# Folding the keys' sums to 64 partitions ahead of one product with ones, in a fused attention and feed-forward kernel

## The chip, the cores and the metric

The kernel runs on one core of one Trainium2 chip. A core has TensorE (PE in the profile; PEld is its weight load), VectorE (DVE), ScalarE (ACT), GpSimd (POOL) and SyncE (SP), which run side by side and wait for each other by semaphores; each takes its own instructions in the order in which they are written. The metric is the device time of one execution in microseconds (us).

## The reference

Linear attention with random features for 8 batches, 8 heads, 576 positions and head size 64, with 128 features, then a feed-forward layer with a residual tanh over 4608 tokens of 512 values:

```python
def phi(x):
    proj = np.einsum('bhsd,md->bhsm', x, omega)
    sq = np.sum(x * x, axis=-1, keepdims=True) / 2.0
    h = proj - sq
    h = h - np.max(h, axis=-1, keepdims=True)
    return np.exp(h) / np.sqrt(m)
q_p, k_p = (phi(q_s), phi(k_s))
kv = np.einsum('bhsm,bhsd->bhmd', k_p, v)
z = np.sum(k_p, axis=2)
num = np.einsum('bhsm,bhmd->bhsd', q_p, kv)
den = np.einsum('bhsm,bhm->bhs', q_p, z)[..., None] + 1e-06
x = num / den                       # then to 4608 x 512
h = x @ w_in                        # 512 -> 2048
out = (h - np.tanh(h)) @ w_out      # 2048 -> 512
```

What matters here is z, the sum over the positions of the keys' features, for each batch, head and feature. It is needed on all 128 partitions, since the denominators are sums over the free dimension of the queries' features times z.

## The kernel before

The tokens are worked on in 9 chunks of 512. The feed-forward layer of one chunk (units f, 16 per chunk) runs while keys and queries of later chunks are prepared. TensorE multiplies in a rounded 32-bit type, so most operands are split into a high part and a low part (the rest), and a product is made of two or three products of parts.

The order of all work is written out by hand in a table of tokens, ORDER. A token names a unit, a step and sometimes buffers: `k20.zh.0` is the step zh of the key unit for batch 2, head pair 0, with buffer 0. The program runs through the table and issues each step's instructions; on each engine they stay in that order. Buffers and PSUM banks are named in the tokens, and waits between engines follow from who writes and reads them.

The first two batches of keys are handled in another form. The other 24 key units (6 batches, 4 head pairs) are made by `k_unit`. In such a unit, 576 positions of two heads are projected, reduced and exponentiated in groups A0, A1, M, B0, B1 (M holds 64 positions of each head, in the two halves of the partitions), multiplied with the values into `pk`, and summed:

- zA and zB (GpSimd, L841 and L842) add the four blocks of a head to `zs`, a place of 128 partitions x 2 heads x 128 features inside the tile `zf`. Each partition holds the sum over the positions that lie on it.
- zM (GpSimd, L846, two instructions of 64 partitions) adds group M.
- zh (VectorE, L851) rounds `zs` to its high part, zl (GpSimd, L854) makes the low part; both stand in the tile `zhl`.
- ca and cv (L858, L861) collect the keys' product with the values out of PSUM.
- kt (TensorE) transposes those (L865) and multiplies a matrix of ones with the high part and with the low part (L867, two products into one PSUM place). That sums over the 128 partitions, with the result on every partition.
- ka, kb, zb, wa, wv take the results out of PSUM.

Other lines of which the text speaks: L682 projections on TensorE (into a PSUM bank that must have been read out before); L693 the reduction on VectorE; L802 and L806 high and low part of the keys' features (VectorE, GpSimd); L820 and L825 those of the values (GpSimd, VectorE); L673 low parts of queries or keys (VectorE); L756, L762, L763, L766, L770 the queries' part with its numerators; L925 the first product of the feed-forward layer (h), L939 tanh and L940 the difference, L929 and L942 its split into zr, L935 to L937 the second product (po); L958 and L960 copy results out.

The tile `zf` is one large tile that holds several things at fixed places: the sums `zs`, the feed-forward layer's working blocks, results that wait to be sent, the identity matrix. So `zf` in a row can be any of these; the line tells which.

Of the kernel before, what the change touches and what calls it, by code (L numbers as in the profile page):

```python
# [127 lines left out]
k32.tM q23.ta0 k32.khA0.1 k32.tA1 q23.z1.5 k32.klA0 k32.eM q23.tv0 x2.h2 f1d.o2 k32.khM.0 q23.a1 k32.kvA0.2 x2.l2 f1e.o1
k32.eA1 q23.l1 f1f.h3 k32.khA1.1 k32.klM q23.m1.6 f1f.th k32.klA1 f1d.o3 q23.ta1 f1f.g k32.vhM.1 k32.kvA1 q23.tv1 f1e.o2
f1f.gh.0 k32.vhB0.0 k32.vlM f1e.o3 x2.h3 k32.zA f20.h0.5 f1f.gl f20.h1 x2.l3 k32.pB0.3 k32.pB1.6 k32.vlB0 k32.cB0  # L130
k32.kvM k33.sa f20.h2 f1f.o0 k32.vhB1.1 k32.tB0 f20.h3 k32.cB1 k32.vlB1 k32.eB0 k33.sv0 k33.lv f21.h0.3 s1.c0.0 k32.tB1
f20.th f21.h1 s1.d0 k32.khB0.1 k33.sv1 k32.eB1 k32.klB0 f21.h2 f20.g k30.ld f21.h3 k32.khB1.0 k32.zB f20.gh.1 k32.kvB0
# [5 lines left out]
q33.p0.0.1 q33.p1.6 q33.c0 f22.o0 q33.c1 q33.t0 k33.kvA1 q33.t1 q33.e0 k33.pB0.0 k33.vhB0.0 f23.h3 k33.vlB0 k33.cB0
q33.d0 q33.e1 k33.pB1.6 f22.o1 k33.tB0 k33.cB1 f23.th k33.tB1 q33.p3.0 k33.kvM k33.eB0 f23.g f22.o2 k33.vhB1.1 q33.c3
k33.vlB1 k33.eB1 q33.p2.6 k33.khB0.0 f22.o3 k30.lv q33.t3 k33.klB0 q33.c2 k33.khB1.1 f23.gh.0 f24.h0.2 k33.zB q33.e3  # L140
q33.t2 k33.kvB0 f23.gl f24.h1 q33.e2 f24.h2 k30.sa k33.klB1 f23.o0 k30.vhA1.0 f23.o1 q30.sa k30.sv0 k33.zM k33.kvB1
f23.o2 k30.vlA1 k33.ca f23.o3 k30.sv1 k30.vhA0.1 k30.pA0.0 f24.h3 k30.cA0 k33.zh.0 k31.ld f25.h0.6 k33.cv f24.th k33.zl
k30.tA0 f25.h1 f24.g k30.eA0 k33.kt k30.vlA0 f24.gh.1 q30.sv f25.h2 k33.ka k33.zb f25.h3 k33.kb k30.pM.0 q32.ld
k30.pA1.2 f24.gl k33.wa f26.h0.3 k30.cM k30.cA1 k30.khA0.1 f25.th k30.tM f24.o0 k30.klA0 q33.d1 k30.eM f24.o1 k30.kvA0.0
f24.o2 k30.khM.0 f25.g k30.vhM.1 f26.h1 k33.wv f25.gh.0 k30.tA1 f24.o3 k30.klM k30.vlM k30.eA1 f26.h2 f25.gl k30.zA
f26.h3 k30.khA1.1 f25.o0 f26.th q33.d3 f25.o1 k30.klA1 f25.o2 f26.g k30.kvA1 k30.pB0.6 k30.vhB0.0 k30.pB1.2 q33.d2
f26.gh.1 f25.o3 k30.vlB0 k30.cB0 q33.rc k30.kvM k31.sa f26.gl f27.h0.3 k30.vhB1.1 q33.n0 f26.o0 q33.n1 k30.vlB1 f27.h1
# [238 lines left out]
def favor_attention_ffn(ctx: ExitStack, tc: tile.TileContext, qT, kT, va, vt, omT, w, out):  # L386
# [395 lines left out]
    def k_unit(b, c):  # L782
# [61 lines left out]
        def z_mid():  # L844
            for h, r in enumerate(halves):
                nc.gpsimd.tensor_add(zs[r, h], zs[r, h], u["phM"][r, 0])  # L846
# [191 lines left out]
```

## Time and profile before

| | |
|---|---|
| median of 3 runs | 1026.26 us (1025.16 to 1032.76) |
| the profiled execution | 1025.03 us, of which the span from the first to the last instruction is 1023.0 us |
| TensorE's granted clock over the span | 0.996 |
| TensorE busy | 1007.6 us (98%) |
| VectorE busy | 780.0 us (76%) |
| ScalarE busy | 685.1 us (67%) |
| GpSimd busy | 329.2 us (32%) |

A row of a group names line, engine, operation, what it writes and reads, shapes and count, then busy time in us, mean length of one in ns, and the engine's idle time just before. A row of a line's or tile's instructions gives minimum, median and maximum length in ns. A row of a timeline gives start and length in us, and in brackets idle time with what ended it; rows that follow each other without a gap are merged (x2). A row of the chain of waits gives the start of a piece of the chain, its length, and the engine and line. A row of a table of stages gives the stretch, its length, and the busy time of TensorE, its weight loads, VectorE, ScalarE and GpSimd. Matmuls are pipelined, so the row of one lasts longer than the time until the next one starts.

The 24 key units of the kind described run from about 155 to 810 us.

### The profile page before, as it was taken

The page shows a single profiled execution, that of the slowest core. Times are in us where ns is not written, and L with a number is a line of the kernel's source. Part 1 is how long each engine was busy: PE and PEld are TensorE (multiplying, and loading weights), DVE is VectorE, ACT ScalarE, POOL GpSimd, SP SyncE. Part 2 cuts the span into 40 slices and gives each one's busy share as a digit, 9 for nine tenths or more (in the row PEclk, how much of TensorE's full clock was granted, in tenths as well). Part 3 has the DMA queues.
Part 4 walks back from the last instruction along what each step waited for, and adds up shares of the span by engine and source line. Part 5 has one row for each costly group of instructions (what it writes and reads, how often), then busy time and mean ns, then how long its engine had stood idle before and what let it go on. Part 6 is the DMA issues. An engine that isn't in the chain of part 4 may idle for free.

```text
span 1023.0 us, 16682 instructions
## 1 busy us (share of the span) xinstructions
PE 1007.6 (98%) x5272; PEld 839.5 (82%) x5272; DVE 780.0 (76%) x2618; ACT 685.1 (67%) x1677; POOL 329.2 (32%) x561
## 2 busy tenths in 40 slices
PE   8799999999999999999999999999999999999998
PEld 7688878888888888888888888888888888888886
DVE  7899768888978898789888997887877868343222
ACT  7977767777866687568676886776856768343222
POOL 2414324552354405550655025512663210000000
PEclk9899999999999999999999999999999999999999
DMA  9944532101111102100220012100210010001001
GB/s 359 412 140 86 141 65 77 54 25 45 42 53 39 34 22 75 47 24 21 65 57 23 24 30 77 36 22 24 76 45 1 22 52 11 1 1 41 1 1 42
DMA packets 24872, 61.78 MB, mean 60 GB/s; under 512 B 2640, under 2 KB 5072, under 8 KB 22736
## 3 DMA queue, kind: packets, MB, share of 16 engines
q1 hardware_dynamic: 23056, 54.81, 16.0%
q0 software_dynamic: 1584, 5.77, 2.9%
q8 instruction: 42, 0.69, 0.3%
q14 instruction: 46, 0.38, 0.1%
q10 hardware_dynamic: 144, 0.13, 0.0%
HBM read 45.50 MB, written 9.44 MB: 54 GB/s over the span
## 4 chain that ended last, share of the span: by engine, by line
PE 86%; DVE 5%; ACT 5%; DMA 2%; POOL 1%; issue 1%; SPq 0%; ACTq 0%; DVEq 0%; POOLq 0%
PE h L925 35%; PE po L935 12%; PE po L937 12%; PE po L936 12%; PE pk_k L834 3%; PE pj_q L682 2%; PE pt_q L748 2%; DMA n_f<-qT 2%; PE pn_q L763 1%; PE pn_q L762 1%; PE pj_k_B L682 1%; ACT phi_q L699 1%; PE pj_k_A L682 1%; DVE zf L730 1%; PE n_pj L554 1%
## 5 line engine op out<-in xcount | busy, mean ns | idle before, releaser
L925 PE MATMUL h<-xa,w 128*128 128x512 f32 x1728 | 440.9, 393 | 0.4 <-DVE nb_k_A L693 0.4
L925 PEld LDWEIGHTS h<-xa,w 128*128 128x128 f32 x1728 | 312.8, 188 | 60.3 <-issue 1.8
L935 PE MATMUL po<-w,zr 128*128 128x512 f32 x576 | 228.3, 396 | 0.0
L937 PE MATMUL po<-w,zr 128*128 128x512 f32 x576 | 225.2, 391 | 0.2 <-DVE zr L942 0.2
L936 PE MATMUL po<-w,zr 128*128 128x512 f32 x576 | 225.0, 391 | 0.0
L942 DVE TENSOR_TENSOR zr<-zf,zr 128x512 fp32r<-128x512 f32 x144 | 106.2, 737 | 69.9 <-ACT zr L929 48.2
L929 ACT CAST zr<-zf 128x512 fp32r<-128x512 f32 x144 | 89.5, 622 | 85.6 <-DVE zf L940 43.8
L940 DVE TENSOR_TENSOR zf<-h,zf 128x512 f32<-128x512 f32 x144 | 98.7, 686 | 54.8 <-ACT zf L939 53.3
L939 ACT ACTIVATE zf<-h 128x512 f32<-128x512 f32 x144 | 85.9, 597 | 76.1 <-PE h L925 49.1
L937 PEld LDWEIGHTS po<-w,zr 128*128 128x128 f32 x576 | 108.1, 188 | 24.6 <-DVE zr L942 0.6
L935 PEld LDWEIGHTS po<-w,zr 128*128 128x128 f32 x576 | 108.3, 188 | 17.4 <-issue 0.3
L936 PEld LDWEIGHTS po<-w,zr 128*128 128x128 f32 x576 | 108.4, 188 | 16.8
L912 POOL TENSOR_TENSOR xa<-xs,xa 128x512 fp32r<-128x512 f32 x16 | 21.3, 1340 | 186.7 <-ACT xa L908 96.7
L699 ACT ACTIVATE phi_q<-phi_q,nb_q 128x128 f32<-128x128 f32 x224 | 75.5, 398 | 4.0 <-DVE nb_q L693 3.0
L806 POOL TENSOR_TENSOR khl_k_A<-phi_Ak,khl_k_A 128x256 fp32r<-128x256 f32 x48 | 37.1, 774 | 123.2 <-DVE khl_k_A L802 115.3
L730 DVE CUSTOM_DVE_ANT_0 zf<-phi_q,zb_k 128x128 bf16<-128x128 f32 (+1 forms) x240 | 66.0, 308 | 2.2 <-ACT phi_q L699 0.6
L693 DVE CUSTOM_DVE_ANT_0 phi_q<-pj_q,phi_q 128x128 f32<-128x128 f32 x224 | 53.6, 284 | 10.5 <-ACT phi_q L688 9.9
L806 POOL TENSOR_TENSOR khl_k_B<-phi_Bk,khl_k_B 128x256 fp32r<-128x256 f32 x48 | 45.5, 947 | 38.6 <-DVE khl_k_B L802 34.0
L688 ACT COPY phi_q<-pj_q 128x256 f32<-128x256 f32 x112 | 39.2, 374 | 19.5 <-PE pj_q L682 18.8
L770 DVE TENSOR_TENSOR xs<-pn_q,xs 64x512 f32<-64x512 f32 x56 | 38.5, 687 | 13.5 <-ACT xs L766 12.3
L766 ACT COPY xs<-pn_q 64x512 f32<-64x512 f32 x56 | 32.6, 582 | 19.2 <-PE pn_q L763 17.8
L756 DVE TENSOR_TENSOR ql_q<-pt_q,qh_q 128x512 fp32r<-128x512 f32 x56 | 38.5, 688 | 8.8 <-ACT qh_q L752 7.8
(151 smaller groups left out, 1726.9 us busy)
## 6 DMA issues: line engine op xcount, KB each, us to landing
raw<-w SPq DMA_DIRECT2D x16, 1024.0 KB, 10.6
...
```

The costliest lines, as they stand in the source:

```text
L693: nc.vector.tensor_tensor_reduce(u[kind][:, at + i], v["pj"][:, i, :M], u[kind][:, at + i], scale=-SCALE, scalar=3.0e38, op0=ALU.add, op1= ...
L699: nc.scalar.activation(u[kind][:, at + i], u[kind][:, at + i], AF.Exp, bias=v["nb"][:, i : i + 1], scale=-1.0)
L730: nc.vector.tensor_tensor_reduce(next(turn)[r], u["ph"][r, i], kvs[b, c][1][r, h], scale=1.0, scalar=EPS, op0=ALU.mult, op1=ALU.add, accum ...
L806: nc.gpsimd.tensor_sub(k[:, :m, 1], u["ph" + g[0]][:, t : t + m], k[:, :m, 0].bitcast(F32))
L925: nc.tensor.matmul(u["p"], w_, x[:, c], start=(c, i) == (0, 0), stop=(c, i) == (NC - 1, 2))
L929: nc.scalar.copy(u["gh"], g)
L935: nc.tensor.matmul(po, u["gh"][:, t], whi, start=f == 0, stop=False)
L936: nc.tensor.matmul(po, u["gh"][:, t], wlo, start=False, stop=False)
L937: nc.tensor.matmul(po, u["gl"][:, t], whi, start=False, stop=f == NF - 1)
L939: st = dict(th=lambda: nc.scalar.activation(g, blocks(u["p"]), AF.Tanh), g=lambda: nc.vector.tensor_sub(g, blocks(u["p"]), g), gh=g_hi, gl ...
L940: g=lambda: nc.vector.tensor_sub(g, blocks(u["p"]), g),
L942: gl=lambda: nc.vector.tensor_sub(u["gl"], g, u["gh"].bitcast(F32)))
```

## The change

A new step zf is put behind zM in all 24 units. VectorE adds partitions 64 to 127 of the sums to partitions 0 to 63 (one instruction of 64 partitions x 256 elements, both inputs in SBUF). The high part is then made of 64 partitions and stands in partitions 0 to 63 of the operand; the low part, of the same 64 partitions, is written to partitions 64 to 127 of the same operand. One product with ones over 128 partitions sums both parts at once, in place of two products. GpSimd's and ScalarE's instructions keep their number and order, TensorE has 24 products fewer, VectorE 24 sums more. All other tokens keep their order; the lines of the table are wrapped anew, so that nearly all of it shows in a diff. Of the table two lines are shown.

```diff
-k20.klB1 f0f.o3 f11.gl k21.ld k22.vhA1.0 k20.kvB1 k20.ca s0.c3.1 f11.o0 f12.th k22.vhA0.1 k20.zM k20.cv s0.d3 k22.pA0.6
...
+k20.klB1 f0f.o3 f11.gl k21.ld k22.vhA1.0 k20.kvB1 k20.ca s0.c3.1 f11.o0 f12.th k22.vhA0.1 k20.zM k20.zf k20.cv s0.d3
...
+        def z_fold():
+            nc.vector.tensor_add(zs[0:D], zs[0:D], zs[D:P])
+
         def z_hi(slot):
             u["zhl"] = ak.tile([P, 2, 2, M], F32R, tag=f"khl{slot}", name=f"zhl_{n}")
             copy = nc.scalar.copy if KH == "A" else nc.vector.tensor_copy
-            copy(u["zhl"][:, 0], zs)
+            copy(u["zhl"][0:D, 0], zs[0:D])
 
         def z_lo():
-            nc.gpsimd.tensor_sub(u["zhl"][:, 1], zs, u["zhl"][:, 0].bitcast(F32))
+            nc.gpsimd.tensor_sub(u["zhl"][D:P, 0], zs[0:D], u["zhl"][0:D, 0].bitcast(F32))
...
-            for i in range(2):
-                nc.tensor.matmul(u["pk"][:, 1].rearrange("p h m -> p (h m)"), ones[:, 0:1].to_broadcast([P, P]),
-                                 u["zhl"][:, i].rearrange("p h m -> p (h m)"), start=i == 0, stop=i == 1)
+            nc.tensor.matmul(u["pk"][:, 1].rearrange("p h m -> p (h m)"), ones[:, 0:1].to_broadcast([P, P]),
+                             u["zhl"][:, 0].rearrange("p h m -> p (h m)"), start=True, stop=True)
...
-        st.update(zA=partial(zsum, 0), zB=partial(zsum, 1), zM=z_mid, zh=z_hi, zl=z_lo, ca=c_hi, cv=c_sum, kt=turned,
+        st.update(zA=partial(zsum, 0), zB=partial(zsum, 1), zM=z_mid, zf=z_fold, zh=z_hi, zl=z_lo, ca=c_hi, cv=c_sum, kt=turned,
```

In the changed kernel's line numbers the fold is L850, and what was L851, L854, L861 and L867 is L855, L858, L865 and L870.

More of the change, by code (lines that the diff above doesn't have):

```diff
@@ L128 @@
[L128 to L132, printed above, removed]
@@ L138 @@
[L138 to L142, printed above, removed]
@@ L143 @@
[L143 to L147, printed above, removed]
@@ new lines @@
+k22.pA0.6 k22.vlA1 f11.o1 k22.vlA0 k22.cA0 f11.o2 k20.zh.0 k22.tA0 k20.zl f11.o3 f12.g k22.eA0 k20.kt f12.gh.1
+k22.khA0.1 k22.pM.6 k22.pA1.5 k22.klA0 k20.ka f12.gl k22.cM k20.zb k22.cA1 q20.d1 f13.th f12.o0 q20.d3 f12.o1 q20.d2
+k20.kb f12.o2 q20.rc k20.wa k22.tM q20.n1 q20.n0 k22.kvA0.3 f12.o3 k20.wv k22.vhM.1 k22.tA1 k22.eM q20.z0.6 f13.g
+k22.eA1 f14.h0.5 k22.khM.0 k22.vlM q20.a0 k22.klM f14.h1 f13.gh.0 k22.zA q20.l0 f14.h2 k22.khA1.1 q20.m0.2 f13.gl
+k22.klA1 q21.p3.6 q20.ta0 f14.h3 q21.c3 q20.tv0 f13.o0 f14.th q21.t3 q20.z1.2 f14.g q21.e3 k22.kvA1 k22.pB0.6 k22.vhB0.0
@@ new lines @@
+f24.o1 k30.kvA0.0 f24.o2 k30.khM.0 f25.g k30.vhM.1 f26.h1 k33.wv f25.gh.0 k30.tA1 f24.o3 k30.klM k30.vlM k30.eA1 f26.h2
+f25.gl k30.zA f26.h3 k30.khA1.1 f25.o0 f26.th q33.d3 f25.o1 k30.klA1 f25.o2 f26.g k30.kvA1 k30.pB0.6 k30.vhB0.0
+k30.pB1.2 q33.d2 f26.gh.1 f25.o3 k30.vlB0 k30.cB0 q33.rc k30.kvM k31.sa f26.gl f27.h0.3 k30.vhB1.1 q33.n0 f26.o0 q33.n1
+k30.vlB1 f27.h1 k30.tB0 k31.lv k31.sv0 f26.o1 k30.cB1 k30.eB0 q33.z0.6 k31.sv1 f27.h2 q33.a0 k30.tB1 k41.ld f26.o2
+k30.khB0.1 k30.eB1 q33.l0 k30.klB0 f27.h3 k30.khB1.0 k30.zB k30.kvB0 f27.th q33.m0.2 f26.o3 f27.g q33.ta0 k31.vhA1.0
@@ new lines @@
+q33.z1.6 k30.klB1 k31.vlA1 f27.gh.0 f28.h0.3 q33.a1 k30.zM k30.zf q33.tv0 k30.kvB1 f28.h1 k30.ca q33.l1 k31.vhA0.1
+q30.p0.2.1 k30.zh.1 f28.h2 k30.cv q30.c0 k30.zl f27.gl q33.m1.6 k30.kt q33.ta1 k31.vlA0 f28.h3 q30.t0 k30.ka k30.zb
+q33.tv1 f27.o0 q30.e0 k30.kb f28.th q30.p1.2 q30.d0 q30.p3.6 k30.wa k31.pA0.0 f28.g q30.c1 f27.o1 q30.c3 k31.cA0 k30.wv
+q30.p2.3 q30.t1 f28.gh.1 f27.o2 k31.tA0 q30.c2 q30.e1 f28.gl k31.pM.2 k31.pA1.0 f27.o3 k31.eA0 q30.t2 q30.d1 f28.o0
+k31.cM q30.e2 f29.h0.3 k31.cA1 k31.tM k31.khA0.0 q32.sa k31.tA1 f29.h1 k31.klA0 q30.t3 f29.h2 q30.d2 q30.e3 q32.sv
@@ new lines @@
+k40.zA f31.o2 f31.o3 f33.h2 f32.gl q41.ld k40.vhM.1 f33.h3 k40.khA1.0 f32.o0 f33.th k40.klA1 k40.vlM f32.o1 k40.kvA1
+k40.pB0.0 f33.g k40.vhB0.0 k40.pB1.6 k40.cB0 k40.kvM k40.vlB0 k43.sa f32.o2 k40.tB0 k40.vhB1.1 k40.vlB1 f32.o3 k43.lv
+f34.h0.7 k40.cB1 k43.sv0 k40.eB0 f34.h1 k43.sv1 f33.gh.0 f34.h2 f33.gl k42.ld f34.h3 k40.tB1 k40.khB0.0 f35.h0.0 k40.eB1
+k40.klB0 f34.th f35.h1 k40.khB1.1 k40.zB f34.g k40.kvB0 f35.h2 f34.gh.1 f35.h3 k43.vhA1.0 f34.gl k40.klB1 f33.o0
+k43.vlA1 f35.th f33.o1 k40.zM k40.zf f35.g k43.pA0.6 k43.pA1.7 k43.cA0 k40.kvB1 f33.o2 k40.zh.0 k43.cA1 k43.vhA0.1
@@ new lines @@
+k43.tA0 k40.ca k40.zl k43.pM.0 k43.vlA0 f33.o3 k43.eA0 k43.cM k40.cv f34.o0 f35.gh.0 k43.tM k43.khA0.1 k40.kt k43.tA1
+k43.eM k43.klA0 f35.gl f34.o1 k43.eA1 k40.ka k43.kvA0.6 k40.zb k43.zA f34.o2 k43.khM.0 f35.o0 k43.khA1.1 f35.o1 k43.klM
+k40.kb k40.wa k43.klA1 f35.o2 k40.wv k43.vhM.1 f34.o3 k43.kvA1 k43.pB0.0 k43.vlM k43.vhB0.0 k43.pB1.7 k43.cB0 f35.o3
+k42.sa k43.tB0 k43.kvM k43.vlB0 f36.h0.2 k43.vhB1.1 k43.vlB1 f36.h1 k43.cB1 k42.sv0 k42.lv k43.eB0 f36.h2 k43.tB1
+k43.khB0.1 f36.h3 k43.eB1 k42.sv1 k43.klB0 f37.h0.0 f36.th k43.khB1.0 k51.ld f37.h1 k43.zB f36.g k43.kvB0 f37.h2
@@ new lines @@
+f36.gh.1 k42.vhA1.0 f37.h3 f36.gl k43.klB1 f38.h0.7 k42.vlA1 f37.th f36.o0 k43.zM k43.zf f37.g k43.kvB1 k42.pA0.2
+f37.gh.0 k42.pA1.0 k42.vhA0.1 k43.zh.1 f36.o1 k43.ca k42.vlA0 k42.cA0 k43.zl f37.gl f36.o2 k42.cA1 f36.o3 k43.cv f38.h1
+k42.tA0 k42.tA1 k42.eA0 k43.kt k42.pM.2 k42.eA1 f38.h2 k42.khA0.0 k42.klA0 k43.ka f38.h3 k42.khA1.1 k43.zb k42.cM k42.zA
+k42.kvA0.0 k43.kb f38.th k42.tM f37.o0 q43.d3 k43.wa k42.eM f37.o1 k42.klA1 f37.o2 k42.khM.0 f37.o3 k42.vhM.1 k43.wv
+f38.g k42.kvA1 k42.pB0.6 q43.d2 f38.gh.1 k42.klM k42.pB1.2 f39.h0.7 k42.cB0 k42.vhB0.0 k51.sa k42.vlM f39.h1 q43.rc
@@ new lines @@
+k42.kvM k42.tB0 f39.h2 q43.n0 k42.vhB1.1 q43.n1 f39.h3 f38.gl q43.z0.6 k42.cB1 k42.vlB1 k42.eB0 f38.o0 k42.tB1 q43.a0
+k42.vlB0 f38.o1 k42.khB0.1 k51.lv k51.sv0 k42.eB1 k42.klB0 f38.o2 f39.th k42.khB1.0 f38.o3 k42.zB q43.l0 k42.kvB0
+f3a.h0.2 f39.g q43.m0.6 k51.sv1 k42.klB1 f39.gh.0 f3a.h1 q43.ta0 f39.gl k50.ld q43.z1.7 k51.vhA1.0 f3a.h2 q43.a1 q43.tv0
+k42.kvB1 k42.zM k42.zf f3a.h3 k42.ca q43.l1 q40.p0.6.1 k42.cv k51.vhA0.1 f3a.th f39.o0 k42.zh.1 q40.c0 k51.vlA1 k42.zl
+f3a.g q43.m1.7 f39.o1 q40.t0 q43.ta1 k51.vlA0 k42.kt q40.e0 q43.tv1 q40.p1.2 q40.p3.6 k42.ka q40.d0 k42.zb q40.p2.7
@@ new lines @@
+k50.khM.0 k51.ca f40.h2 s3.d2 k50.cA0 k50.vhA0.1 k50.cA1 f40.h3 k50.tA0 k50.klM k51.cv k50.eA0 f41.h0.3 k50.vlA1
+k50.vlA0 f40.th s3.c3.1 k51.kt f41.h1 f40.g s3.d3 k51.ka k51.zb k51.kb f41.h2 f40.gh.1 k50.khA0.1 k50.tA1 k50.klA0
+k51.wa f41.h3 f40.gl k50.eA1 k50.kvA0.2 f42.h0.1 k50.zA k50.khA1.1 f41.th f40.o0.6 f41.g f40.o1.5 k50.klA1 k51.wv
+f41.gh.0 f40.o2.0 k50.vhM.1 f41.gl k50.kvA1 k50.pB0.7 k50.pB1.4 k50.cB0 f41.o0 k50.vhB0.0 k53.sa k50.vlM f41.o1 k50.tB0
+k50.kvM k50.vlB0 f41.o2 k50.cB1 k53.sv0 k50.vhB1.1 k50.eB0 f40.o3.3 k50.tB1 k50.vlB1 f41.o3 k50.eB1 k53.sv1 k53.lv
@@ new lines @@
+q60.sv k60.cA1 f4e.o2 f4f.gh.0 f4e.o3 k60.eM k60.tA1 q61.ld k60.khM.0 f51.h0.2 k60.eA1 f4f.gl k60.klM q62.d2 f51.h1
+f50.th k60.zA f4f.o0 f4f.o1 f50.g s4.c0.0 k60.khA1.1 f4f.o2 f50.gh.1 s4.d0 s4.c1.1 k60.klA1 f4f.o3 f50.gl s4.d1 k60.kvA1
+k60.pB0.7 k60.vhB0.0 k60.pB1.1 k60.cB0 f50.o0.6 k60.vlB0 k62.sa k60.tB0 k60.kvM f50.o1.5 k60.vhB1.1 s4.c3.0 f50.o2.7
+k60.cB1 k60.vlB1 k60.eB0 s4.d3 k62.sv0 f50.o3.3 k62.lv s4.c2.1 k62.sv1 f51.h2 s4.d2 k60.tB1 f51.h3 k63.ld k60.khB0.1
+k60.eB1 f52.h0.0 k60.klB0 f51.th k60.khB1.0 f52.h1 k60.zB f51.g k60.kvB0 f52.h2 f51.gh.0 k62.vhA1.0 f52.h3 f51.gl
@@ new lines @@
+f53.gh.0 k62.vlB1 f54.h2 k62.eB1 k62.khB0.1 k63.lv f53.gl k62.klB0 f54.h3 k62.khB1.0 f53.o0 f54.th k62.zB k63.sv1
+k62.kvB0 f53.o1 f53.o2 f54.g k61.ld f53.o3 k63.vhA1.0 f54.gh.1 k62.klB1 k63.vlA1 f55.h0.1 k62.zM k62.zf f54.gl k62.kvB1
+k63.pA0.2 k62.ca k63.pA1.4 k63.cA0 f55.h1 k62.cv k63.cA1 k63.tA0 k63.vhA0.1 f55.h2 k62.zh.1 k63.eA0 k63.vlA0 k62.zl
+k63.tA1 k63.pM.2 f55.h3 k63.cM k63.khA0.0 k63.eA1 k62.kt k63.tM k63.klA0 f55.th f54.o0 k63.khA1.1 k62.ka k63.zA k62.zb
+k62.kb k63.kvA0.4 k63.eM f55.g f54.o1 k62.wa k63.khM.0 f55.gh.0 f54.o2 k63.klA1 k62.wv f54.o3 k63.klM f55.gl k63.kvA1
@@ new lines @@
+q62.ta1 q60.d0 q60.p1.0 f57.h3 k63.ka q62.tv1 q60.c1 k63.zb f56.o2 k63.kb f57.th q63.d3 k63.wa q60.p3.1 q60.t1 q60.p2.4
+q60.c3 q63.rc f56.o3 k63.wv q60.c2 q63.n0 q63.n1 f58.h0.0 q60.t2 q60.t3 f58.h1 q60.e2 f57.g q63.z0.4 q60.e3 q60.d2
+f58.h2 q63.a0 q60.d3 k61.pA0.1 q60.e1 f58.h3 q63.l0 f57.gh.0 q60.d1 f59.h0.2 k61.cA0 f57.gl q61.sa q63.m0.4 q60.rc
+f57.o0 k61.tA0 q60.n0 q60.n1 q63.z1.1 q61.sv f59.h1 f57.o1 q63.a1 q63.ta0 q63.l1 f59.h2 q70.ld f58.th q63.tv0 f57.o2
+k61.eA0 f58.g q63.m1.1 k61.khA0.0 q61.p0.4.1 f58.gh.1 q60.z0.0 k61.klA0 q63.ta1 f59.h3 f58.gl q60.a0 f57.o3 q63.tv1
```

425 lines of the change are left out of this document (193 added, 232 removed).

## The prediction

> **What bounds the kernel now.** I read the page's busy times and its chain first, then the busy time by stage, then the chain of waits around one edited place, then the timelines of sampled places.
>
> ```profile
> PE 1007.6 (98%) x5272; PEld 839.5 (82%) x5272; DVE 780.0 (76%) x2618; ACT 685.1 (67%) x1677; POOL 329.2 (32%) x561
> PE 86%; DVE 5%; ACT 5%; DMA 2%; POOL 1%; issue 1%; SPq 0%; ACTq 0%; DVEq 0%; POOLq 0%
> 160.00:400.00 240.00, 239.01 (x1226) 199.60 (x1225) 206.93 (x770) 179.55 (x462) 101.20 (x181) 1.00 0.16 47
> 600.00:810.00 210.00, 209.63 (x1073) 177.35 (x1072) 170.76 (x633) 146.44 (x375) 91.95 (x162) 1.00 0.12 38
> ```
>
> TensorE (PE) sets the time: 98% busy, 86% of the chain. Between 160 and 810 us, where all 24 edited units lie, it shows almost no idle time (columns of the stage rows: PE, weight loads, VectorE, ScalarE, GpSimd busy). But a matmul's row lasts longer than its turn, so small waits hide in that busy time, and VectorE (DVE) is loaded too: 206.93 of 240 us. The chain at the first edited place, unit k20, tells more:
>
> ```profile
> 179.88 0.42 POOL zf L846
> 180.35 0.67 DVE vhl_k_A L825 x2
> 181.03 0.28 DVE zhl_k L851
> 181.73 0.61 DVE zf L940
> 182.36 0.63 ACT zr L929
> 183.02 0.93 DVE zr L942
> 183.99 0.50 PE po L937
> ```
>
> Here the time runs not through PE but from GpSimd's (POOL's) sum L846 through VectorE and ScalarE to the matmul L937. At this place nothing covers a microsecond added to VectorE.
>
> **What is removed: one product with ones per unit.**
>
> ```profile
> 182.49 0.48 PE L867 MATMUL pk_k<-zhl_k,ones 128*128 128x256 f32 x2
> 182.81 0.28 PE L682 MATMUL pj_k_M<-om,x_k 128*128 128x256 f32 x1
> ```
>
> The two products last 0.48 us together, one such product 0.28, so the second starts 0.20 after the first: 24 x 0.20 = 4.8 us of PE time at most. It counts only until PE's next wait for another engine, as at L937 above, so its worth lies between 0 and 4.8. I take 40%, 1.9 us, since the places below show VectorE's results ending several of PE's waits.
>
> The Trainium skill ("TensorE: Matmul & The Clock Gate", section "Wait — 56ns, not 53.3ns?") gives a warm matmul its columns over 2.4 GHz and about 2.5 ns. For 256 columns that is an estimate of 0.109 us, 2.6 us for 24, and by it the term would be 1.0 instead of 1.9. The trace's 0.20 decides.
>
> **What is added: a fold on VectorE that waits for GpSimd.** Each unit gets one sum of 64x256 with both inputs in SBUF. Its length is bounded by the sums of two SBUF inputs with 128 and 512 elements per partition:
>
> ```profile
> L825 DVE TENSOR_TENSOR vhl_k_A<-v_k,vhl_k_A x48: 275/292/850, 157.3 to 772.3; 128x128 fp32r<-128x128 f32 x48
> L942 DVE TENSOR_TENSOR zr<-zf,zr x144: 640/693/1680, 65.1 to 1013.3; 128x512 fp32r<-128x512 f32 x144
> L846 POOL TENSOR_TENSOR zf<-zf,phi_mk x48: 449/462/981, 179.8 to 798.8; 64x128 f32<-64x128 f32 x48
> ```
>
> Between 0.28 and 0.69 us (minimum/median/maximum stand in ns); a third of the way gives 0.41 for 256 elements. Alone that is 24 x 0.41 = 10 us of VectorE time in a stretch that has 20% idle.
>
> The larger part is where it stands. VectorE takes its instructions in order, and the fold is put right behind GpSimd's sums in the written order, so everything behind it waits for them. Before, the first reader, L851, came later:
>
> ```order
> L958 COPY zf_68<-po_0_3_942 128x512
> L861 TENSOR_TENSOR c1_k2_0_2028<-pk_k2_0_1898,c1_k2_0_2028 128x256
> L825 TENSOR_TENSOR vhl_k2_2_A1_2024<-v_k2_2_1986,vhl_k2_2_A1_2024 128x2x64
> L825 TENSOR_TENSOR vhl_k2_2_A0_2035<-v_k2_2_1986,vhl_k2_2_A0_2035 128x2x64
> L851 CAST zhl_k2_0_2054<-zf_68 128x256
> ```
>
> That is VectorE before, around k20's split of the sums (zhl). And after:
>
> ```order
> L961 COPY zf_68<-po_0_3_942 128x512
> L850 TENSOR_TENSOR zf_68<-zf_68 64x256
> L865 TENSOR_TENSOR c1_k2_0_2028<-pk_k2_0_1898,c1_k2_0_2028 128x256
> L826 TENSOR_TENSOR vhl_k2_2_A1_2024<-v_k2_2_1986,vhl_k2_2_A1_2024 128x2x64
> L826 TENSOR_TENSOR vhl_k2_2_A0_2035<-v_k2_2_1986,vhl_k2_2_A0_2035 128x2x64
> L855 CAST zhl_k2_0_2055<-zf_68 64x256
> ```
>
> The fold (L850) has moved the dependence on GpSimd three instructions forward; the sum c1 and both value splits now queue behind it. At k30 (326 us) it is the same with other work behind it, xs and ql:
>
> ```order
> L826 TENSOR_TENSOR vhl_k3_1_A1_3823<-v_k3_1_3767,vhl_k3_1_A1_3823 128x2x64
> L850 TENSOR_TENSOR zf_68<-zf_68 64x256
> L771 TENSOR_TENSOR xs_97<-pn_q3_3_0_3813,xs_97 64x512
> L757 TENSOR_TENSOR ql_q3_3_1_3850<-pt_q3_3_1_3825,qh_q3_3_1_3837 128x512
> L855 CAST zhl_k3_0_3857<-zf_68 64x256
> ```
>
> Without the L850 row this is the row order before.
>
> To price the wait I take every sixth of the 24 places: units k20, k30, k51, k63. In the timelines below (start, length, engine, line) the POOL rows are the two sums L846, and the first DVE row at a place is what the fold now stands in front of, except where said.
>
> ```profile
> 434.95 1.04 POOL L846 TENSOR_TENSOR zf<-zf,phi_mk 64x128 f32<-64x128 f32 x2
> 436.03 0.29 DVE L851 CAST zhl_k<-zf 128x256 fp32r<-128x256 f32 x1 [0.22 <-POOL zf L846]
> 325.92 0.51 DVE L825 TENSOR_TENSOR vhl_k_A<-v_k,vhl_k_A 128x128 fp32r<-128x128 f32 x1
> 179.84 1.12 POOL L846 TENSOR_TENSOR zf<-zf,phi_mk 64x128 f32<-64x128 f32 x2
> 180.01 0.43 DVE L861 TENSOR_TENSOR c_k<-pk_k,c_k 128x256 f32<-128x256 f32 x1 [0.35 <-ACT c_k L858]
> 326.25 1.04 POOL L846 TENSOR_TENSOR zf<-zf,phi_mk 64x128 f32<-64x128 f32 x2
> 326.36 0.67 DVE L770 TENSOR_TENSOR xs<-pn_q,xs 64x512 f32<-64x512 f32 x1
> 327.99 0.40 PE L682 MATMUL pj_q<-om,x_q 128*128 128x256 f32 x2
> 498.04 0.98 POOL L846 TENSOR_TENSOR zf<-zf,phi_mk 64x128 f32<-64x128 f32 x2
> 499.10 0.74 POOL L806 TENSOR_TENSOR khl_k_B<-phi_Bk,khl_k_B 128x256 fp32r<-128x256 f32 x1
> 500.22 0.29 DVE L693 CUSTOM_DVE_ANT_0 phi_mk<-pj_k_M,phi_mk 128x128 f32<-128x128 f32 x1 [1.81 <-ACT phi_mk L688]
> 656.11 0.98 POOL L846 TENSOR_TENSOR zf<-zf,phi_mk 64x128 f32<-64x128 f32 x2
> 656.72 0.93 DVE L942 TENSOR_TENSOR zr<-zf,zr 128x512 fp32r<-128x512 f32 x1
> 659.09 0.41 DVE L861 TENSOR_TENSOR c_k<-pk_k,c_k 128x256 f32<-128x256 f32 x1
> 659.65 0.41 PE L865 MATMUL pk_k<-zf,c_k 128*128 128x128 f32 x2
> ```
>
> From the first three rows: VectorE starts 0.03 after GpSimd's sums end (435.99 to 436.03), and starts its next instruction 0.07 before the last one ends (326.43 against 326.36). So the work behind a fold starts 0.03 + 0.41 - 0.07 = 0.37 us after the sums end, if VectorE stood waiting, or 0.34 later than now if it didn't.
>
> - k20: sums end 180.96, next work would start 181.33 instead of 180.01: 1.32 late. The chain quoted first runs through this work without a gap to PE, so PE loses 1.3.
> - k30: sums end 327.29, L770 would start 327.66 instead of 326.36: 1.30 late. Its end frees the PSUM bank for the projection at 327.99, which now has 327.99 - 327.03 = 0.96 us; some 0.05 of it is the signal's way, so PE loses 0.4.
> - k51: sums end 499.02, but VectorE idles until 500.22: nothing lost.
> - k63: L942 ends at 657.65, after the sums (657.09), so only 0.34 is added. The transposes at 659.65 need L861's result of 659.50; with 0.05 for the signal 0.10 is free, and PE loses 0.24.
>
> Together 1.94 us at four places out of 2.96 us of VectorE's delay (two thirds passes on), six times that for 24: 11.6 us. Per place the bounds are 0 and 1.3, so 0 and 31 us.
>
> **What else moves.** z_hi and z_lo work on 64 partitions; L846 (64 partitions, 128 elements) takes 0.46 like the full-height sums beside it, so I count no gain. One edit relieves: L846 takes up to 0.98 us instead of 0.46 where VectorE's two-input sums run beside it, and a VectorE that stands behind the fold no longer does that. The page of groups bounds it:
>
> ```profile
> L846 POOL TENSOR_TENSOR zf<-zf,phi_mk 64x128 f32<-64x128 f32 x48 | 25.9, 540 | 1.8
> ```
>
> 48 x (540 - 462) ns = 3.7 us over all, two thirds of which would reach PE: 0 to 2.5. Some of that blocking comes from work ahead of the fold and stays; I take 0.7.
>
> **Sum.** +11.6 - 1.9 - 0.7 = +9.0 us. The profiled execution took 1025.03 us (span 1023.0), the median of three runs 1026.26. So 1034 for an execution like the profiled one and **1035.3 us** against the median, 0.9% slower. Below 1% (1016 to 1036.5) a measurement of this kernel hardly tells a change from none.
>
> **Rivals.**
>
> The fold is hidden, and the kernel is a little faster. VectorE idles 20 to 25% of its time, and PE has work queued, so delays of about a microsecond are taken up before a matmul needs the result, as at k51. Then 1026.3 less 2 to 4.8 is 1021.5 to 1024. It decides where most results have over 1.3 us to spare; against it three of four places stand. Chance 0.16.
>
> Contention makes it worse. The fold reads two SBUF inputs while GpSimd goes on to its next instruction, and such pairs hold each other up: L942 takes 640 to 1680 ns, L846 449 to 981. At k51 L806 (0.74) follows the sums by 0.08 us. If GpSimd gets in first, the fold waits up to 0.74; with half of that, 0.37, at 24 places and two thirds passing on, 24 x 0.37 x 0.67 = 6 us more: 1041. Against it: the fold should start some 0.05 us before L806. Chance 0.17.
>
> The Trainium skill ("SBUF — State Buffer", section "Who interferes with whom") says that a VectorE instruction with two SBUF inputs and a GpSimd instruction that reads SBUF exclude each other, and the first blocks the second completely. By that rule the fold pays or GpSimd does, but one of them always; the trace's stretched rows agree.
>
> The product frees nothing. PE's turns may be set by VectorE at the kt step anyway, and the 4.8 us go into the next wait. Then 1026.3 + 11.6 - 0.7 = 1037. Chance 0.12.
>
> **How the numbers follow.** Forecast 0.55, spread by the sampling of four places to some 1028 to 1040. Hidden 0.16, contention 0.17, nothing freed 0.12. The range 1025 to 1042 leaves out most of the hidden case and the top of the contention case. Slower by over 1% (above 1036.5): all of the contention case, two thirds of the nothing-freed case, 0.4 of the forecast's: 0.47. Faster by over 1% would need 10 us where 4.8 are removed: 0.02. Within 1%: 0.51.
>
> **What would show it.** Right: a fold row of about 0.41 us; VectorE idle ahead of it in some 20 places, ended by POOL zf, about 0.9 us each; PE waits at k20 and at the projection of k30 grown by about 1 and 0.4 us; a single product in the place of L867's pair, the next matmul 0.20 earlier behind it. Wrong: folds that start with no idle time ahead; a fold of 0.7 us or more; GpSimd's rows behind the sums longer by the fold's length with PE waiting for them; or PE's busy time down by 4.8 us and the span with it.

## The result and the profile after

The changed kernel takes 1036.95 us (median of six runs, 1035.91 to 1045.02) where the kernel before, run beside it, takes 1025.81 (1025.16 to 1032.76). The ratio is 1.0111, with a 95% interval of 1.0084 to 1.0138: 11.1 us slower, where 9.0 slower (1035.3) was forecast. Now and then an execution of either kernel is 6 to 8 us longer, at a lower clock (1045.02 at 0.986 of full speed over the span, the others of that kernel at 0.994 to 0.996); ratios take these in and medians hardly do, and in the table of the experiments the two differ by up to 2 us.

The profiled execution is the slowest of the six: 1045.02 us, span 1043.2. Its extra 8 us lie in the first stage, before the first fold, as the clock's row (PEclk) and the rows by stage show. First the page: busy times, clock, shares of the chain.

```profile
PE 1020.4 (98%) x5248; PEld 844.8 (81%) x5248; DVE 784.0 (75%) x2642; ACT 684.5 (66%) x1677; POOL 330.2 (32%) x561
PEclk8699999999999999999999999999999999999999
PE 73%; DVE 10%; ACT 7%; POOL 6%; issue 2%; DMA 2%; ACTq 0%; POOLq 0%; SPq 0%; DVEq 0%
```

Then the rows by stage (stretch, its length, busy time of PE, weight loads, VectorE, ScalarE and GpSimd, granted clock, DMA share, GB/s); the first stage of the kernel before stands by itself.

```profile
0.00:160.00 160.00, 150.88 (x990) 123.15 (x991) 133.61 (x333) 124.55 (x285) 52.09 (x69) 0.98 0.60 194
```

```profile
0.00:160.00 160.00, 151.15 (x948) 123.90 (x949) 127.00 (x317) 117.62 (x271) 47.21 (x65) 0.91 0.61 192
160.00:400.00 240.00, 236.76 (x1195) 195.71 (x1194) 203.65 (x748) 175.12 (x446) 99.49 (x177) 1.00 0.15 42
600.00:810.00 210.00, 207.56 (x1053) 173.68 (x1052) 170.59 (x615) 145.73 (x370) 87.06 (x155) 1.00 0.13 38
```

The clock is 0.91 up to 160 us, where it was 0.98, and 1.00 behind it. GpSimd's sums of the first changed unit, k20, start at 188.86 us against 179.84 before: 9.0 late before the change can act.

```profile
188.86 0.99 POOL L847 TENSOR_TENSOR zf<-zf,phi_mk 64x128 f32<-64x128 f32 x2
```

The span is 20.2 longer, so 11.2 us arise behind that point, which agrees with the 11.1 of the medians. So positions inside this profile are compared from one event to the next, not by their time from the start.

In the two later stages shown, PE's idle time went from 0.99 to 3.24 us and from 0.37 to 2.44. In the chain, PE fell from 86% to 73%, VectorE rose from 5 to 10% and GpSimd from 1 to 6%. The groups of the edited lines (busy, mean ns of one, idle time just before, and what ended it):

```profile
L850 DVE TENSOR_TENSOR zf<-zf 64x256 f32<-64x256 f32 x24 | 10.1, 421 | 21.2 <-POOL zf L847 21.2
L847 POOL TENSOR_TENSOR zf<-zf,phi_mk 64x128 f32<-64x128 f32 x48 | 24.5, 511 | 1.8
L870 PE MATMUL pk_k<-zhl_k,ones 128*128 128x256 f32 x24 | 8.8, 367 | 0.9 <-POOL zhl_k L858 0.9
```

The fold lasts 0.42 us, and VectorE stands idle 21.2 us ahead of the 24 folds, all of it waiting for GpSimd's sums. Before, its wait for these sums was 0.4 us in all. At k20 the chain of waits (start, length, engine and line) now reads:

```profile
189.38 0.47 POOL zf L847
189.86 0.02 issue
189.88 0.04 DVE zf L850
189.92 0.31 issue
190.22 0.41 DVE c_k L865
190.64 0.40 DVE vhl_k_A L826 x2
191.04 0.21 DVE zhl_k L855
...
191.66 0.61 DVE zf L943
192.29 0.63 ACT zr L932
192.95 0.99 DVE zr L945
193.98 0.50 PE po L940
```

The sum c1 (L865), which before ran beside GpSimd's sums, stands in the chain behind them, and so does all that follows. From the end of the sums to the last matmul of the chain there were 183.99 - 180.96 = 3.03 us; now there are 193.98 - 189.85 = 4.13. The two value splits (L826), which before ran beside the sums and took 0.67 of the chain, run behind them now and take 0.40. Over all 48 splits of this kind the mean fell from 444 to 389 ns, 2.6 us of VectorE's time.

The other three sampled places, in the timeline: GpSimd's two sums, the fold behind them, and the row that tells what became of the delay.

```profile
337.81 1.04 POOL L847 TENSOR_TENSOR zf<-zf,phi_mk 64x128 f32<-64x128 f32 x2
338.88 0.42 DVE L850 TENSOR_TENSOR zf<-zf 64x256 f32<-64x256 f32 x1 [0.89 <-POOL zf L847]
339.96 0.51 PE L683 MATMUL pj_q<-om,x_q 128*128 128x256 f32 x2 [0.23 <-DVE xs L771]
514.46 0.98 POOL L847 TENSOR_TENSOR zf<-zf,phi_mk 64x128 f32<-64x128 f32 x2
515.48 0.42 DVE L850 TENSOR_TENSOR zf<-zf 64x256 f32<-64x256 f32 x1 [0.65 <-POOL zf L847]
515.52 0.98 POOL L807 TENSOR_TENSOR khl_k_B<-phi_Bk,khl_k_B 128x256 fp32r<-128x256 f32 x1
516.64 0.29 DVE L694 CUSTOM_DVE_ANT_0 phi_mk<-pj_k_M,phi_mk 128x128 f32<-128x128 f32 x1 [0.74 <-ACT phi_mk L689]
676.13 0.42 DVE L850 TENSOR_TENSOR zf<-zf 64x256 f32<-64x256 f32 x1
678.57 0.41 PE L869 MATMUL pk_k<-zf,c_k 128*128 128x128 f32 x2 [0.26 <-DVE c_k L865]
```

At k30 the projection starts 339.96 - 338.85 = 1.11 us behind the sums' end where it started 327.99 - 327.29 = 0.70 behind it: 0.41 lost. At k51 VectorE still idles 0.74 behind the fold, and nothing is lost. At k63 the fold starts without a wait, and the transposes wait 0.26 us that they did not wait before.

Last, the single product at k20 and the matmul behind it.

```profile
192.17 0.38 PE L870 MATMUL pk_k<-zhl_k,ones 128*128 128x256 f32 x1 [0.40 <-POOL zhl_k L858]
192.39 0.28 PE L683 MATMUL pj_k_M<-om,x_k 128*128 128x256 f32 x1
```

The next matmul starts 0.22 after the product, where it started 0.32 after the first of two (182.49 and 182.81). Over all 24 places the medians are 0.203 and 0.319: taking away one product brings it 0.116 nearer, not 0.20. That is the turn of the second product before: 0.117 from its start to the next matmul's, by the same count.

### The profile page after: what moved, and what is told of

It reads as the page before. It is cut to its first block, busy times and chain, and to the rows that moved or that the text cites. A ratio compares the mean times of both kernels' runs of the same rounds, so it can differ in the third digit from the quotient of the medians.

```text
span 1043.2 us, 16687 instructions
## 1 busy us (share of the span) xinstructions
PE 1020.4 (98%) x5248; PEld 844.8 (81%) x5248; DVE 784.0 (75%) x2642; ACT 684.5 (66%) x1677; POOL 330.2 (32%) x561
## 4 chain that ended last, share of the span: by engine, by line
PE 73%; DVE 10%; ACT 7%; POOL 6%; issue 2%; DMA 2%; ACTq 0%; POOLq 0%; SPq 0%; DVEq 0%
PE h L928 29%; PE po L938 10%; PE po L940 10%; PE po L939 10%; POOL khl_k_B L807 2%; PE pj_q L683 2%; PE pk_k L835 2%; PE pt_q L749 2%; POOL zf L847 1%; ACT x_k L671 1%; PE k_pk L495 1%; PE pn_q L764 1%; POOL zt_k L842 1%; PE pn_q L763 1%; DVE zf L943 1%
## 5 line engine op out<-in xcount | busy, mean ns | idle before, releaser
L945 DVE TENSOR_TENSOR zr<-zf,zr 128x512 fp32r<-128x512 f32 x144 | 106.9, 742 | 70.0 <-ACT zr L932 47.9
L807 POOL TENSOR_TENSOR khl_k_A<-phi_Ak,khl_k_A 128x256 fp32r<-128x256 f32 x48 | 37.9, 789 | 119.0 <-DVE khl_k_A L803 94.4
L807 POOL TENSOR_TENSOR khl_k_B<-phi_Bk,khl_k_B 128x256 fp32r<-128x256 f32 x48 | 46.3, 965 | 38.7 <-DVE khl_k_B L803 34.1
L683 PEld LDWEIGHTS pj_q<-om,x_q 128*128 128x128 f32 x224 | 36.5, 188 | 9.4 <-DVE xs L771 1.4
```

Source lines behind the costliest of these rows:

```text
L683: nc.tensor.matmul(v["pj"][:, i], x, om2, start=True, stop=True)
L807: nc.gpsimd.tensor_sub(k[:, :m, 1], u["ph" + g[0]][:, t : t + m], k[:, :m, 0].bitcast(F32))
L945: gl=lambda: nc.vector.tensor_sub(u["gl"], g, u["gh"].bitcast(F32)))
```

## The experiments

The theory on record was the place: VectorE's in-order wait, with other work queued behind it, costs the time. Its rivals were the fold's length (VectorE time as such, and the conflicts it makes with GpSimd) and a larger or smaller worth of the product. The times of experiments are medians; ratios are against runs of the kernel before on the same chip, whose medians were 1025.6, 1025.97 and 1025.99 us.

| kernel | median us | over before, us | ratio (95%) |
|---|---|---|---|
| the changed kernel | 1036.95 | +11.1 | 1.0111 (1.0084 to 1.0138) |
| fold late | 1031.13 | +5.5 | 1.0046 (1.0030 to 1.0062) |
| a wait alone, first form | 1033.53 | +7.9 | 1.0071 (1.0046 to 1.0095) |
| a wait alone | 1032.83 | +6.9 | 1.0058 (1.0036 to 1.0081) |
| a sum alone, no wait | 1027.56 | +2.0 | 1.0002 (0.9980 to 1.0024) |
| one product, no fold | 1024.56 | -1.0 | 0.9982 (0.9963 to 1.0002) |
| fold, product made twice | 1038.14 | +12.2 | 1.0121 (1.0092 to 1.0149) |
| early at six dear places | 1034.80 | +8.8 | 1.0078 (1.0048 to 1.0108) |
| early at six cheap places | 1030.73 | +4.8 | 1.0043 (1.0022 to 1.0064) |
| fold when the sums are there | 1029.18 | +3.2 | 1.0030 (1.0008 to 1.0053) |
| a sum alone ahead of zh | 1027.79 | +1.8 | 1.0015 (0.9991 to 1.0040) |
| sums made sooner | 1038.82 | +12.8 | 1.0116 (1.0083 to 1.0149) |

**The fold right ahead of its reader.** The same fold, with its token moved behind the work that queued behind it.

```diff
-... k20.zM k20.zf k20.cv s0.d3 k22.pA0.6 k22.vlA1 f11.o1 k22.vlA0 k22.cA0 f11.o2 k20.zh.0 ...
+... k20.zM k20.cv s0.d3 k22.pA0.6 k22.vlA1 f11.o1 k22.vlA0 k22.cA0 f11.o2 k20.zf k20.zh.0 ...
```

> The changed kernel with the fold moved in the written order from right behind GpSimd's sums to right ahead of the high part (zh), its first reader. Everything else as in the changed kernel. Theory 'place' (VectorE stands behind GpSimd's sums and with it all that is queued there): VectorE no longer stands waiting, only 0.42 us of work is added at a spot that depends on the sums anyway; 0 to 2 us over the kernel before. Rival 'length' (the fold's own 24 x 0.42 us of VectorE time and its conflicts with GpSimd over SBUF inputs cost the time, wherever it stands): 8 us or more over the kernel before.

Half of the loss went and half stayed: 5.5 us, which neither expectation had. Below are the group of folds and, from the timeline at k30, the rows from the fold to the product (line numbers are 5 higher than in the changed kernel).

```profile
L855 DVE TENSOR_TENSOR zf<-zf 64x256 f32<-64x256 f32 x24 | 10.1, 422 | 1.1 <-POOL zf L852 0.4
...
329.94 0.42 DVE L855 TENSOR_TENSOR zf<-zf 64x256 f32<-64x256 f32 x1
330.39 0.29 DVE L860 CAST zhl_k<-zf 64x256 fp32r<-64x256 f32 x1
330.83 1.38 POOL L863 TENSOR_TENSOR zhl_k<-zf,zhl_k 64x256 fp32r<-64x256 f32 x1 [1.03 <-DVE zhl_k L860]
330.94 0.67 DVE L950 TENSOR_TENSOR zr<-zf,zr 128x512 fp32r<-128x512 f32 x1
332.26 0.38 PE L875 MATMUL pk_k<-zhl_k,ones 128*128 128x256 f32 x1 [0.53 <-POOL zhl_k L863]
```

The idle time ahead of the folds is gone, so the wait is not what remains. Here the high part is 0.45 us later for the fold, and the low part, 0.72 at k30 of the changed kernel, takes 1.38 beside VectorE's sum L950 of two SBUF inputs. The product waits 0.53 for it. Since it reads both parts in one operand, it cannot begin with the high part, as the first of the two products could.

**The wait alone, first form.** The kernel before, with one small VectorE copy of a value out of the sums in the fold's place.

```diff
+            nc.vector.tensor_copy(small("zw", 1, f"zw_{n}", 1)[0:D], zs[0:D, 1, 0:1])
```

> The kernel before, with one added VectorE instruction per unit right behind GpSimd's sums: a copy of one element per partition out of the sums to a place that nobody reads. Both products stay. So the wait is there without the fold's length and without the saved product. Theory 'place': the wait alone makes most of the loss, 5 to 8 us over the kernel before. Rival 'length': 0 to 1 us.

7.9 us, but the run doesn't measure what it was made for. The value copied isn't one that zM writes, and in the trace the copy waited for GpSimd at one place only, 0.4 us; and the small new tile moved the tiles behind it (zr, zf, the weights) by 32 bytes. PE's products h became slower over the whole kernel, also behind 810 us, where no key unit is left (0.251 us of busy time each against 0.246). The groups of h, before and then this run:

```profile
L925 PE MATMUL h<-xa,w 128*128 128x512 f32 x1728 | 440.9, 393 | 0.4 <-DVE nb_k_A L693 0.4
```

```profile
L934 PE MATMUL h<-xa,w 128*128 128x512 f32 x1728 | 448.1, 398 | 0.4 <-DVE nb_k_A L699 0.3
```

7.2 us more for the same 1728 products. The run is left out of the argument.

**The wait alone.** The copy now reads a value that zM writes and puts it into a place that exists already, so that no tile moves; 64 partitions of one element.

```diff
+            nc.vector.tensor_copy(junk.bitcast(BF16)[D:P, 0:1], zs[D:P, 1, 0:1])
```

> As the run with the wait only, with two things mended: the copied element is one that GpSimd's last sum writes (partitions 64 to 127 of the second head), so that all 24 places wait for it, and it goes to a place inside a tile that is there already, so that no tile changes its address. Both products stay. Theory 'place': 5 to 8 us over the kernel before (the sampled places by the prediction's working with 0.1 us in place of 0.41 give 1.0, 0.1, 0 and 0 us, times six: 6). Rival 'length': 0 to 1 us.

The group of the copies:

```profile
L855 DVE CAST zf<-zf 64x1 bf16<-64x1 f32 x24 | 3.7, 154 | 20.7 <-POOL zf L852 20.6
```

The idle time is that of the changed kernel (20.6 against 21.2 us), and the mean row of h is back at 393 ns. It costs 6.9 us (6.0 by the ratio, 3.7 to 8.3 by its interval), within the 5 to 8 of the place theory: the wait alone, with nothing folded and both products kept, makes up most of the loss. The length theory, which leaves the wait out, is rejected.

**A sum alone.** A sum of constants of the fold's size in the fold's place, which waits for nothing; the two products stay.

```diff
+            o = om2.bitcast(F32)
+            nc.vector.tensor_add(junk.bitcast(BF16)[0:D], o[0:D], o[0:D])
```

> The kernel before, with a sum of 64x256 elements with two SBUF inputs at the fold's place, made of constant data so that it waits for nobody, and written where nobody reads. Both products stay. The fold's length without its wait. Theory 'place': 0 to 2 us over the kernel before, since VectorE's idle time takes it up. Rival 'length': 8 us or more.

```profile
L856 DVE TENSOR_TENSOR zf<-om 64x256 bf16<-64x256 f32 x24 | 14.6, 610 | 0.1
```

It lies beside GpSimd's sums, takes 0.61 us in the mean where the fold takes 0.42, and still costs only 2.0 us by the medians and nothing by the ratio. VectorE's free time takes up a sum that waits for nothing.

**One product alone.** The kernel before with the product of the low part left out, so the sums lack their low part; no fold, no wait.

```diff
-            for i in range(2):
+            for i in range(1):
```

> The kernel before with only the product of the high part (the low part is made but not multiplied in, so that part of the keys' sums is left out). No fold. The worth of a product by itself. If a product costs 0.20 us of PE's time and all of it counts: 4.8 us under the kernel before. If it costs what lies between the second product and the next matmul in the trace of before, 0.117 us: up to 2.8 us under it. If PE's turns there are set by other engines: no change.

1.0 us faster by the medians, 1.8 by the ratio, with 3.8 at the end of the interval. So 24 products aren't worth 4.8.

**The fold with the product made twice.** The changed kernel, its single product issued twice into the same place.

```diff
+            for i in range(2):
-            nc.tensor.matmul(...zhl[:, 0]..., start=True, stop=True)
+                nc.tensor.matmul(...zhl[:, 0]..., start=True, stop=True)
```

> The changed kernel with the product with ones done twice, the second time over the first (both start afresh, so the result is the same). The fold and its wait stay, the saved product is given back. If a product is worth 0.20 us with 40% of it counting, 1.9 us over the changed kernel; if it is worth 0.117 us, 1.1 us, and at most 2.8; if it frees nothing, no difference. So 11 to 14 us over the kernel before.

1.2 us over the changed kernel, by medians of two sets of runs whose kernels before are 0.16 apart: some 40% of 24 x 0.117 = 2.8. The intervals of the two kernels overlap, so the size of this difference is uncertain. The fold without the gain of a product is thus +12.2.

**Early at six places only, dear or cheap.** The late fold, but with the changed kernel's early place at k20, k21, k23, k41, k43 and k52 in one kernel, and at k22, k32, k51, k50, k73 and k70 in the other. The places were chosen by what PE lost there in the two traces. The diff shows k20, one of the dear six.

```diff
-... k20.zM k20.cv s0.d3 k22.pA0.6 k22.vlA1 f11.o1 k22.vlA0 k22.cA0 f11.o2 k20.zf k20.zh.0 ...
+... k20.zM k20.zf k20.cv s0.d3 k22.pA0.6 k22.vlA1 f11.o1 k22.vlA0 k22.cA0 f11.o2 k20.zh.0 ...
```

> The kernel with the late fold, but at six units (k20, k21, k23, k41, k43, k52) the fold stands early, as in the changed kernel. These are the six at which the working by rows gives the most (1.0 to 1.3 us each, 7.2 together). If the loss hangs on what PE has to spare at each place: 3 to 6 us over the late fold, 8 to 11 over the kernel before. If each early fold costs about the same: 1.5 us over the late fold, 6.5 over the kernel before.

> The kernel with the late fold, but at six units (k22, k32, k51, k50, k73, k70) the fold stands early, as in the changed kernel. These are the six at which the working by rows, done for every place, gives the least loss (0 to 0.13 us each). If the loss hangs on what PE has to spare at each place: 0 to 1 us over the late fold. If each early fold costs about the same (11 us in all, 0.45 each, against 0.2 for a late one): 1.5 us over it.

The folds of the dear six and then of the cheap six:

```profile
L855 DVE TENSOR_TENSOR zf<-zf 64x256 f32<-64x256 f32 x24 | 10.1, 421 | 7.1 <-POOL zf L852 6.6
```

```profile
L855 DVE TENSOR_TENSOR zf<-zf 64x256 f32<-64x256 f32 x24 | 10.2, 423 | 4.9 <-POOL zf L852 4.3
```

The dear six add 6.0 us of idle time over the late fold's 1.1 and cost 3.7 us more than it (3.3 by the ratios, 3 to 6 expected); the cheap six add 3.8 us of idle time and cost nothing more (-0.4; 0 to 1 expected). VectorE's idle time is thus no measure of the loss. The places had been picked by whether PE soon needs the work queued behind the wait, and that told dear from cheap.

**The fold when the sums are there.** At each place the token stands where, by the trace of before, VectorE would first find the sums done: not in front of work that could have run, and no later than ahead of the high part, where it still ends up at six places.

```diff
-... k30.zM k30.zf q33.tv0 k30.kvB1 f28.h1 k30.ca q33.l1 k31.vhA0.1 q30.p0.2.1 k30.zh.1 ...
+... k30.zM q33.tv0 k30.kvB1 f28.h1 k30.ca k30.zf q33.l1 k31.vhA0.1 q30.p0.2.1 k30.zh.1 ...
```

> The changed kernel with each unit's fold put at the first point of VectorE's order at which, by the trace of before, GpSimd's sums are done (no earlier than behind them, no later than ahead of the high part). 5 of 24 folds come out right ahead of the high part as in the run with the late fold, the others 1 to 20 steps earlier. Theory 'both ends cost' (too early and VectorE stands waiting; too late and the low part reaches the product with ones late): 1 to 4 us over the kernel before, under the late fold's 4.7. Rival (the fold's length and its conflicts with GpSimd cost the same wherever it stands without a wait): 4.7 again.

```profile
L855 DVE TENSOR_TENSOR zf<-zf 64x256 f32<-64x256 f32 x24 | 11.5, 478 | 6.1 <-POOL zf L852 5.6
```

3.2 us: the best order of the fold that was tried, 8 us better than the changed kernel's and, by its interval, still slower than no fold. The places went by the trace of before; in this kernel's own trace the folds still wait 5.6 us.

**A sum alone ahead of the high part.** The sum of constants again, now where the late fold stands; nothing depends on it. The diff is against the run of the sum alone.

```diff
-... k20.zM k20.zf k20.cv ... f11.o2 k20.zh.0 ...
+... k20.zM k20.cv ... f11.o2 k20.zf k20.zh.0 ...
```

> The kernel before with the sum of constant data (64x256, two SBUF inputs, nobody waits for it) put right ahead of the high part instead of behind GpSimd's sums. Both products stay. If the late fold is dear because 0.4 us more on VectorE there make the low part late for the product with ones: 3 to 6 us over the kernel before. If it is dear because the high part depends on the fold: 1 to 2 us, as the same sum at the earlier place (2.0 by the medians).

1.8 us. VectorE's time at that place, and the high part's delay by it, are in this figure. The late fold costs 5.5, though it has a product fewer. By the expectation, 1 to 2 us means that the late fold is dear because the high part depends on it; but this run also lacks the product that needs both parts at once, and the low part in its new form. How the rest divides between these isn't settled. In the trace, the wait for the low part ahead of the products (weight load's side) was nothing before, 0.4 us here and 2.4 with the late fold:

```profile
L877 PEld LDWEIGHTS pk_k<-zhl_k,ones 128*128 128x128 f32 x48 | 7.3, 190 | 0.4 <-POOL zhl_k L864 0.4
```

```profile
L875 PEld LDWEIGHTS pk_k<-zhl_k,ones 128*128 128x128 f32 x24 | 4.5, 188 | 2.4 <-POOL zhl_k L863 2.4
```

Another piece shows in the traces: what GpSimd does behind that low part comes late too. PE's weight loads wait for the low parts of the keys' A groups (L812) 1.2 us here and 3.9 with the late fold:

```profile
L840 PEld LDWEIGHTS pk_k<-khl_k_A,vhl_k_A 128*128 128x128 f32 x96 | 17.5, 188 | 5.0 <-POOL khl_k_A L812 1.2 <-POOL khl_k_M L812 0.5
```

```profile
L840 PEld LDWEIGHTS pk_k<-khl_k_A,vhl_k_A 128*128 128x128 f32 x96 | 17.0, 188 | 7.3 <-POOL khl_k_A L812 3.9 <-POOL khl_k_M L812 0.5
```

Before, this wait was 1.8 us, with the wait alone 1.1, in the changed kernel 2.8 and with the fold when the sums are there 3.2. The late fold with two products of 64 partitions each, the first of which could start on the high part, wasn't tried.

**The sums made sooner.** The other way out of the wait: the changed kernel, with GpSimd's zM moved ahead of the low parts of the last key group, right behind zB.

```diff
-... k20.zB k20.khB1.1 ... k20.klB1 ... k22.vhA0.1 k20.zM k20.zf k20.cv ...
+... k20.zB k20.zM k20.khB1.1 ... k20.klB1 ... k22.vhA0.1 k20.zf k20.cv ...
```

> The changed kernel with GpSimd's last sums (zM) moved ahead, right behind zB, so that they are done when VectorE comes to the fold, which stands where it stands in the changed kernel. GpSimd's low parts of the last key groups come about 1 us later for it. If VectorE's wait is what costs: most of the 11 us goes, 1 to 5 us over the kernel before, of which the delayed low parts may make up the most. If the fold's length costs: 8 us or more.

A miss: 12.8 us, no better than the changed kernel. VectorE's wait did fall, to 5.0 us, but PE waits for the low parts that zM was moved past. The fold's group and the product with those low parts; then that product in the kernel before:

```profile
L855 DVE TENSOR_TENSOR zf<-zf 64x256 f32<-64x256 f32 x24 | 12.9, 537 | 5.4 <-POOL zf L852 5.0
...
L840 PE MATMUL pk_k<-khl_k_B,vhl_k_B 128*128 128x256 f32 x96 | 20.5, 300 | 6.8 <-POOL khl_k_B L812 6.8
```

```profile
L834 PE MATMUL pk_k<-khl_k_B,vhl_k_B 128*128 128x256 f32 x96 | 19.0, 284 | 0.3 <-POOL khl_k_B L806 0.3
```

0.3 us of waiting became 6.8. GpSimd is busy a third of the time over the span, but here PE needs its next work as soon as VectorE's.

## Why the prediction was right

**The bound.** PE behind VectorE at the edited places: kept. PE's share of the chain fell, VectorE's and GpSimd's rose, and in the stretch of the key units the clock is 1.00 in both.

**The fold's length.** 0.41 us was worked out, 0.42 measured, in all 24 places alike (420 to 424 ns). The "20% idle" of VectorE beside it was high: its own stage rows give 14 and 19% between 160 and 810 us.

**The fold's wait.** Some 20 places at about 0.9 us were expected; 23 places, 21.2 us, 0.92 each. The four sampled places, in us:

| unit | forecast for PE | measured |
|---|---|---|
| k20 | 1.3 | 1.10 |
| k30 | 0.4 | 0.41 |
| k51 | 0 | 0 |
| k63 | 0.24 | 0.26 |
| sum times six | 11.6 | 10.6 |

At k20 PE lost less than forecast because the value splits, no longer beside GpSimd's sums, were shorter (0.40 for 0.67); the prediction had counted such a relief for GpSimd only.

The term with its relief was 11.6 - 0.7 = 10.9; the run with the product made twice puts it at 12.2, with the ends of its interval at 9.4 and 15.3. Its make-up fits as far as it was measured. The wait alone is 6.9. In the changed kernel the work behind it is late by the fold's length too: an estimate from the rows is 23 places x (0.42 - 0.15 of the copy) x two thirds = 4.1, together 11.0. A sum that doesn't stand behind a wait costs 0 to 2, so the length costs much only where idle time has just been used up. The prediction had no term for the low parts that GpSimd makes behind the fold: PE's weight loads wait 1.4 us for those of the sums (nothing before) and 2.8 for those of the A groups (1.8 before). The runs do not show how far this is VectorE's delay passed on. That four places with losses from 0 to 1.3 give the sum of 24 to within some 2 us is in part luck.

**The relief of GpSimd.** The 48 sums lost 29 ns each (540 to 511), 1.4 us of blocking, two thirds of which is 0.9; 0.7 was taken. No run tells its share of the time.

**The product: the mis-sized step.** "The second starts 0.20 after the first: 24 x 0.20 = 4.8" took the distance between the two products for the price of one. The first stands behind the transposes L865 and has the longer turn (its row starts 0.03 after that of the second transpose, so part of the transpose may lie in it); what is saved is the turn of the second, 0.117 us, 2.8 for 24. With the 40% that the prediction let count the term is -1.1, not -1.9; the two runs on it gave 1.2 and 1.0. So the matmul behind the single product starts 0.10 (k20) to 0.116 (median) earlier, not 0.20: 0.20 was the wrong row for the purpose. The prediction let it decide against 0.109, its estimate from the Trainium skill ("TensorE: Matmul & The Clock Gate", section "Wait — 56ns, not 53.3ns?"). The measured turn, 0.117, lies close to that estimate.

With -1.1 for -1.9 the sum is +9.8 in place of +9.0, against +11.1 measured. What is left, 1.3 us, lies inside the sampling of four places and the interval.

**The rivals.** Hidden (1021.5 to 1024) fell: one place of four hides the delay, and even the best order of the fold is above the kernel before. Contention (1041) fell as the price of the fold itself: no fold is longer than 424 ns, and GpSimd's next instruction waited instead. At k51 its low part took 0.98 us, not 0.74, and PE did not notice. That one side of such a pair pays is what the Trainium skill states ("SBUF — State Buffer", section "Who interferes with whom"), and the trace agrees: the low part of 1.38 beside L950 and the sum of constants at 0.61 beside GpSimd's. But at one place at least the rival holds. Behind k40's sums the low part L807 now takes 1.44 beside VectorE's sum L945 (0.68), where before it took 0.74 and VectorE's sum 1.09, and PE waits for it:

```profile
436.93 1.44 POOL L807 TENSOR_TENSOR khl_k_A<-phi_Ak,khl_k_A 128x256 fp32r<-128x256 f32 x1 [1.06 <-PE pk_k L869]
437.11 0.68 DVE L945 TENSOR_TENSOR zr<-zf,zr 128x512 fp32r<-128x512 f32 x1
438.42 0.30 PEld L835 LDWEIGHTS pk_k<-khl_k_A,vhl_k_A 128*128 128x128 f32 x2 [1.20 <-POOL khl_k_A L807]
```

The same pair falls out the same way in the runs of the late fold and of the fold when the sums are there, so about 1 us of each may be contention, not the 6 of the rival.

That the product frees nothing (1037) can't be told from the forecast by the time of the changed kernel, 1036.95; the two runs on the product give 1.0 and 1.2 us, and neither interval by itself excludes zero.

**Chances.** 0.47 stood on slower by over 1% and 0.51 on less; 1.0111 lies just above the line, and its interval on both sides.
